# Gathering four blocks at a time instead of three, with two of them by way of DRAM

## The chip, the core and the metric

The kernel runs on one NeuronCore of a Trainium2 chip. The metric is the device time of one launch in microseconds (us). Three runs of the kernel before took 2212.91, 2213.55 and 2214.76 us; the median is 2213.55 us.

## What is computed

The input is x, 4 sequences of 4096 tokens with 192 features, in float32. Three steps follow each other.

```python
# 1. a causal convolution over 7 tokens, weights softmax-normed per head
out[b, s, h, g] = sum_k w[h, k] * x_pad[b, s + k, h, g]
# 2. first network, w_in 192 x 2048 and w_out 2048 x 192
h = x @ w_in;  x = (h - tanh(h)) @ w_out
# 3. second network, other weights of the same sizes
h = maximum(x @ w_in, 0);  out = (h * h) @ w_out
```

All weights and results are wanted to float32 accuracy, so most products are made from parts: a value is split into a rounded high part and the rest, and three matmuls (high x high, low x high, high x low) stand for one product.

## The kernel before

**Blocks and units.** The 16384 tokens are cut into NBLK = 32 blocks of T = 512. The hidden layer of 2048 is cut into 16 tiles of 128 features. A unit (network m, block b, pair p) makes two of the 16 hidden tiles from z, the block's input, and multiplies two hidden tiles of the unit three places earlier (LAG = 3) with the second weights. There are 8 units to a block, and 512 in all. `units` (lines 692 to 698) is their order: blocks 0 and 1 in turn, blocks 2 to 29 one by one, blocks 30 and 31 in turn, then the second network block by block.

**Parts A and B.** The 192 output features are part A (the first 128) and part B (the last DB = 64). Part A goes through the split matmuls inside the units (line 526). Part B is made by plain float32 matmuls (lines 500 and 507) with 64 columns, of which two lie side by side on the engine. They need all 16 hidden tiles of a block in SBUF, so they are gathered: run in one go, after the last unit of a group of blocks.

**Gathering.** The hidden tiles of 128 x 512 float32 (256 KB) lie in a ring of RING = 32 slots, just two blocks' worth. `gather_at` (lines 700 to 705) says after which unit `gathered` (line 1039) comes. Blocks 0 and 1 are gathered in two parts. From then on three blocks make a group, ten groups in each network; blocks 30 and 31 of the second network come at the very end. Of three blocks the first is in `sent_away`: each of its tiles goes to DRAM right after it is made (`send_away`, line 511), and its slot is free again. The other two stay. When the group is complete, `gathered` issues 16 products for the kept pair (`products_b`: one hidden tile of both blocks at a time, line 500). Each frees two slots, into which two tiles of the first block are fetched from DRAM (`fetch`, line 515, DMAs on SP's queue). Eight products follow for the block alone (`products_b_alone`: two hidden tiles of one block at a time, line 507), whose two half sums are then added.

**Finishing.** `finish_b` (line 640) takes a pair's sum out of PSUM into the one ub buffer (by ScalarE in the first network, line 650, by VectorE in the second, line 648) and stores it: one DMA to DRAM as y in the first network (line 654), four DMAs into the output in the second (lines 656 to 659). `finish_b_alone` (line 663) does so for a single block, by a copy, an add and, in the second network, a transposition. The last pair of all is gathered in two pieces of 384 and 128 tokens, and half of its stores go by ScalarE's queue; line 658 picks the pair by its number.

**Order of the work.** The order on each engine is written out ahead by a planner (lines 708 to 1180). Each piece of work is a Job with an engine (PE, DVE, ACT, or SP for DMAs), an assumed time, and the jobs and buffers that it needs. PE's jobs stay in the order in which `build` writes them: each needs the one before it (line 756). `set_late` (line 1112) gives PE's jobs due times from their assumed times and works back from them to the others. `emit_all` (line 1149) then plays the plan through: each engine takes, among what could start soonest, the job with the earliest due time. Each engine, and SP's queue, runs its instructions in that order on the chip.

**Input of a block.** In the first network VectorE convolves block by block (lines 289 to 295), part A for one block and part B for two, and z is split by ScalarE and VectorE (lines 379 to 404); a DMA copies one half of z (line 371). In the second network y is loaded back from DRAM (lines 426 to 432). There are two z buffers.

**Weights.** The weights come as 64-bit floats and are decoded by ScalarE and VectorE (`decode_ops`, line 130). The eight parts of the second network's weights are loaded late (`late_loads`, lines 1093 to 1094): the first after unit 0 of block 28 of the first network, and each further one 3 units later. There are WBUFS = 9 buffers; all but one of the eight wait for one that block 31 of the first network has used for the last time.

Of the kernel before, what the change touches and what calls it, by code (L numbers as in the profile page):

```python
# [34 lines left out]
def conv_mlp_mlp_kernel(ctx: ExitStack, tc: tile.TileContext, x, weight, w_in1, w_out1, w_in2, w_out2, out):  # L35
# [13 lines left out]
    nc = tc.nc  # L49
# [6 lines left out]
    T = 512  # L56
# [583 lines left out]
    def finish_b(m, b, lo=0, hi=T):  # L640
        box = {}

        def take():
            if lo == 0:
                last_ub[:] = [op.tile([P, T], F32, name="ub")]
            ub = box["ub"] = last_ub[0]
            if m:
                nc.vector.transpose(ub[:, lo:hi], acc_b[m, b, lo][:, lo:hi])  # L648
            else:
                nc.scalar.copy(ub, acc_b[m, b, lo])  # L650

        def send():
            if m == 0:
                nc.sync.dma_start(out=far_pair(b), in_=box["ub"])
                return
            for i in range(2):
                for j in range(4, D // 32):
                    q = nc.scalar if b == NBLK - 2 and i else nc.sync
                    store(j, b + i, box["ub"], 32 * (j - 4) + i * DB, q, lo, hi)

        return [take, send]
# [35 lines left out]
    for b in range(NBLK):  # L697
        units += one_block(1, b)
    at = {u: i for i, u in enumerate(units)}
    gather_at = {5: (0, [0, 1], 0, 6), 15: (0, [0, 1], 6, NU)}  # L700
    sent_away = set()
    for m in range(2):
        for b in range(2 - 2 * m, NBLK - 2 * m, 3):
            gather_at[at[m, b + 2, NP - 1]] = m, [b, b + 1, b + 2], 0, NU
            sent_away.add((m, b))
    pairs = [(m, p) for m in range(2) for p in range(NP)]

    class Buffer:
# [163 lines left out]
    def build():  # L872
# [139 lines left out]
                steps_2(k, v, makes, uses, 0)  # L1012
                step.append(pe(lambda k=k, run=run: run(k), 0.2267, wants[k], makes, uses))
        finish(*v[:2], step[5], step[5])
        gathered(1, [NBLK - 2, NBLK - 1], 0, NU)

    def wants_2(wants, v):
        hi, lo_ = ready_w[v[0], v[2]][2:]
# [20 lines left out]
    def gathered(m, blocks, lo, hi):  # L1039
        b = blocks[-2]  # L1040
        ub = Buffer("ub")
        start = len(in_order)
        for piece in [(0, T)] if (m, b) != (1, NBLK - 2) else [(0, LAST), (LAST, T)]:
            share = (piece[1] - piece[0]) / T
            if lo == 0:
                sum_b[m, b] = Buffer("pB")
            q = sum_b[m, b]
            for f in range(lo, hi):
                us = [(m, b + i, f // 2) for i in range(2)]
                needs = [t_done[u, f % 2] for u in us]  # L1050
                if piece[1] == T:
                    free_slots.extend(t_of[u, f % 2].slot for u in us)
                j = pe(lambda f=f, piece=piece: products_b(m, b, f, *piece), 0.8586 * share + 0.19 * (f in (lo, hi - 1)), needs, [] if f else [q], [*(t_of[u, f % 2] for u in us), *([q] if f else [])])
            if hi < NU:
                return
            take, send = finish_b(m, b, *piece)
            j = (dve if m else sca)(take, 0.62 if m else 0.5, [j], [] if piece[0] else [ub], [q, *([ub] if piece[0] else [])])
            y_kept["B", b] = y_kept["B", b + 1] = dma(send, 4 if m else 1, [j], (), [ub])
        if len(blocks) == 2:
            return  # L1060
        a = blocks[0]
        fetched = []
        for f in range(NU):
            t = slot_of_ring()
            fetched.append((dma(lambda f=f, t=t: fetch(m, a, f, t.slot), 1, [away[(m, a, f // 2), f % 2], in_order[start + f // 2]], [t], (), lag=2.5), t))
        q = Buffer("pB")
        for p in range(NP):
            (j0, t0), (j1, t1) = fetched[2 * p : 2 * p + 2]
# [7 lines left out]
            j = dve(turn[0], 0.62, [j], (), [ub])  # L1076
        y_kept["B", a] = dma(send, 2 if m else 1, [j], (), [ub])

    away = {}
    LAST = 384  # L1080
    sum_b = {}
    t_of, t_done, acc_of = {}, {}, {}
# [8 lines left out]
        todo.setdefault(i, []).append(b)  # L1091
    g_bufs = {}
    for n in range(NP, 2 * NP):
        late_loads[at[0, NBLK - 4, 0] + 3 * (n - NP)] = n

    def finish(m, b, done_1, done_0):
        p0, p1 = (acc_of[m, b, i] for i in range(2))
# [113 lines left out]
```

## Time and profile before

| | |
|---|---|
| median of 3 runs | 2213.55 us (2212.91 to 2214.76) |
| profiled execution | 2213.45 us |
| its span, first to last instruction | 2211.7 us |
| PE (TensorE) busy | 2203.8 us |
| DVE (VectorE) busy | 1562.6 us |
| ACT (ScalarE) busy | 1535.0 us |
| moved by DMA | 245.79 MB |

The profile is that of one execution. PE is TensorE's matmuls, PEld its weight loads, SP the engine that issues DMAs; SPq is its queue. A name such as `pB<-ring,wb` says which tile an instruction writes and which it reads; t is a hidden tile in DRAM, ring one in SBUF. L500 is line 500 of the kernel. Each plain float32 matmul stands in the trace as two, so 4 of them make one product of the text.

### The profile page before, as it was taken

To read this page: it belongs to the slowest core of one execution; us is meant where nothing else is said; L and a number is where in the kernel's file an instruction comes from. 1 tells how busy PE (TensorE), PEld (TensorE's weight loads), DVE (VectorE), ACT (ScalarE), POOL (GpSimd) and SP (SyncE) were. 2 spreads that over 40 slices of the span, in tenths; PEclk is the share of its full clock that TensorE was granted. 3 is DMA by queue.
4 is the path that set the end of the run, shared out by engine and by line. 5 is a ranking of instruction groups with operands and counts; after the bars stand their busy time and mean duration, and the time that the engine had idled before them with its cause. 6 is when DMAs were issued, how large, how long until landed. Compare 5 with 4: busy or idle time off the path is not lost.

```text
span 2211.7 us, 45057 instructions
## 1 busy us (share of the span) xinstructions
PE 2203.8 (100%) x17530; PEld 1610.0 (73%) x17530; DVE 1562.6 (71%) x2479; ACT 1535.0 (69%) x2715; POOL 3.3 (0%) x21
## 2 busy tenths in 40 slices
PE   9999999999999999999999999999999999999999
PEld 6786776768686867678786868686867767686867
DVE  9997978879796979698854646464646556464644
ACT  8775766757575757576785858585857668585855
POOL 0000000000000000000000000000000000000000
PEclk9999999999999999999999999999999999999999
DMA  5315243333425241545433332424152433333230
GB/s 145 101 44 186 65 146 110 108 103 106 138 83 158 63 165 46 183 114 180 140 107 108 101 122 87 150 58 165 39 184 69 140 105 99 108 102 125 85 92 16
DMA packets 319549, 245.79 MB, mean 111 GB/s; under 512 B 211853, under 2 KB 219109, under 8 KB 319333
## 3 DMA queue, kind: packets, MB, share of 16 engines
q1 hardware_dynamic: 318245, 242.77, 35.6%
q8 instruction: 137, 2.24, 0.4%
q14 instruction: 79, 0.65, 0.1%
q10 hardware_dynamic: 1088, 0.13, 0.0%
HBM read 125.90 MB, written 109.05 MB: 106 GB/s over the span
## 4 chain that ended last, share of the span: by engine, by line
PE 97%; DVE 1%; DMA 1%; SPq 1%; ACT 0%; issue 0%; DVEq 0%; ACTq 0%
PE ph L526 46%; PE p L526 31%; PE pB L500 13%; PE pB L507 6%; DMA st<-in_moe_w_out 0%; SPq L118 0%; DMA ring<-in_moe_w_in 0%; DVE accA L295 0%; DMA st<-in_moe_w_in 0%; DVE gl L602 0%; DVE ring L585 0%; DVE da L160 0%; DVE accB L295 0%; SPq L285 0%; ACT da L144 0%
## 5 line engine op out<-in xcount | busy, mean ns | idle before, releaser
L526 PE MATMUL ph<-z,w 64*128 64x512 f32 (+1 forms) x9198 | 1747.5, 387 | 1.5 <-DVE z L375 1.0
L526 PEld LDWEIGHTS ph<-z,w 64*128 64x128 f32 (+1 forms) x9198 | 1415.9, 184 | 192.8 <-issue 16.9
L526 PE MATMUL p<-gh,w 64*128 64x512 f32 x4096 | 1255.0, 387 | 0.6 <-DVE w L181 0.6
L602 DVE TENSOR_TENSOR gl<-ring,gh 128x512 fp32r<-128x512 f32 x1024 | 668.9, 687 | 265.8 <-ACT gh L596 247.8
L526 PEld LDWEIGHTS p<-gh,w 64*128 64x128 f32 x4096 | 749.5, 184 | 78.0 <-DVE w L181 1.0
L526 PE MATMUL p<-gl,w 64*128 64x512 f32 x2048 | 788.4, 386 | 0.0
L580 ACT ACTIVATE ring<-ph 128x512 f32<-128x512 f32 x1024 | 607.5, 599 | 218.7 <-PE ph L526 182.8
L596 ACT CAST gh<-ring 128x512 fp32r<-128x512 f32 x1024 | 606.3, 616 | 74.4 <-DVE ring L585 65.1
L526 PEld LDWEIGHTS p<-gl,w 64*128 64x128 f32 x2048 | 375.8, 184 | 38.7 <-DVE gl L602 0.3
L585 DVE TENSOR_TENSOR ring<-ph,ring 128x512 f32<-128x512 f32 x512 | 332.2, 681 | 27.8 <-ACT ring L580 27.2
L500 PE MATMUL pB<-ring,wb 128*64 128x512 f32 (+2 forms) x1472 | 307.8, 575 | 0.0
L500 PEld LDWEIGHTS pB<-ring,wb 128*64 128x64 f32 x1472 | 102.8, 137 | 193.5 <-issue 191.3
L587 DVE TENSOR_TENSOR ring<-ring,ph 128x512 f32<-128x512 f32 x256 | 175.8, 687 | 55.0 <-ACT ring L580 51.5
L668 ACT COPY ub<-pB 64x512 f32<-64x512 f32 x20 | 11.7, 584 | 232.7 <-PE pB L507 231.9
L589 ACT ACTIVATE ring<-ring 128x512 f32<-128x512 f32 x256 | 161.8, 632 | 7.4
L507 PE MATMUL pB<-ring,wb 128*64 128x512 f32 x640 | 140.7, 592 | 0.0
L672 DVE TENSOR_TENSOR ub<-pB,ub 64x512 f32<-64x512 f32 x20 | 13.7, 683 | 171.3 <-ACT ub L668 171.3
L295 DVE SCALAR_TENSOR_TENSOR accA<-xTa,taps,accA 128x512 f32<-128x512 f32 x180 | 133.5, 741 | 0.7
L507 PEld LDWEIGHTS pB<-ring,wb 128*64 128x64 f32 x640 | 46.0, 137 | 91.4 <-issue 83.9
L648 DVE STREAM_TRANSPOSE ub<-pB 128x512 f32<-128x512 f32 (+2 forms) x12 | 8.1, 673 | 108.3 <-PE pB L500 108.3
L295 DVE SCALAR_TENSOR_TENSOR accB<-xTb,taps,accB 128x512 f32<-128x512 f32 x90 | 67.1, 745 | 0.2 <-ACT accB L292 0.2
L388 ACT CAST z<-accA 128x512 fp32r<-128x512 f32 x30 | 18.6, 621 | 54.4 <-DVE accA L295 47.3
(99 smaller groups left out, 474.0 us busy)
## 6 DMA issues: line engine op xcount, KB each, us to landing
t<-ring SPq DMA_DIRECT2D x320, 256.0 KB, 2.1
ring<-t SPq DMA_DIRECT2D x320, 256.0 KB, 5.3
ya<-tu SPq DMA_DIRECT2D x32, 256.0 KB, 2.1
accA<-ya SPq DMA_DIRECT2D x32, 256.0 KB, 2.7
accB<-yb SPq DMA_DIRECT2D x64, 128.0 KB, 2.7
out<-ua SPq DMA_DIRECT2D x128, 64.0 KB, 1.9
xa<-in_x SPq DMA_DIRECT2D x120, 64.0 KB, 2.4
z<-z SPq DMA_DIRECT2D x30, 256.0 KB, 2.9
```

What stands on the lines that cost most here:

```text
L295: nc.vector.scalar_tensor_tensor(a, t[:, k : k + T], w, a, op0=ALU.mult, op1=ALU.add)
L388: nc.scalar.copy(zt[:, 0, 0], acc["A", b])
L500: nc.tensor.matmul(acc_b[m, b, lo][half(i), lo:hi], w, ring_t[m, b + i, f][:, lo:hi], start=f == 0, stop=f == NU - 1)
L507: nc.tensor.matmul(acc_b[m, b, "alone"][half(i)], weights_b(m, p)[:, i], ring_t[m, b, 2 * p + i], start=p == 0, stop=p == NP - 1)
L526: ins = nc.tensor.matmul(o, w, r, start=start, stop=stop).ins
L580: nc.scalar.activation(t, ph, AF.Relu if m else AF.Tanh)
L585: nc.vector.tensor_tensor(t, ph, t, op=ALU.subtract)
L587: nc.vector.tensor_tensor(t, t, ph, op=ALU.mult)
L589: nc.scalar.activation(t, t, AF.Square)
L596: nc.scalar.copy(gh, t_t[m, b, f])
L602: nc.vector.tensor_tensor(gl, t_t.pop((m, b, f)), gh.bitcast(F32), op=ALU.subtract)
L672: nc.vector.tensor_tensor(ub, acc_b[m, b, "alone"][half(0)], ub, op=ALU.add)
```

## The change

Groups have three or four blocks, by the lists N0 and N1. In the first network, from block 2 on, they are 3, then six times 4, then 3; in the second, seven times 4, then 2 and 2. All but the last two blocks of a group are sent away. `gathered` handles the last two as before; one block ahead of them is handled as before; two blocks go to the new `gathered_pair`, which asks for two tiles after each product of the kept pair and then makes 16 products for the fetched pair, in the way of a kept pair, with its own take into ub and its own store. The assumed time of a fetch in the plan rises from 0.55 to 0.66 us. The late loads keep their first place; the second comes after unit 1 of block 29, and each further one 3 units later, which is 6 units later than before for seven of the eight. The constant ENDS replaces NBLK - 2 where the last pair is meant.

```diff
--- before.py
+++ after.py
@@ -655,7 +655,7 @@
                 return
             for i in range(2):
                 for j in range(4, D // 32):
-                    q = nc.scalar if b == NBLK - 2 and i else nc.sync
+                    q = nc.scalar if b == ENDS and i else nc.sync
                     store(j, b + i, box["ub"], 32 * (j - 4) + i * DB, q, lo, hi)
 
         return [take, send]
@@ -697,12 +697,17 @@
     for b in range(NBLK):
         units += one_block(1, b)
     at = {u: i for i, u in enumerate(units)}
+    ENDS = NBLK - 2
+    N0, N1 = [3] + [4] * 6 + [3], [4] * 7 + [2, 2]
     gather_at = {5: (0, [0, 1], 0, 6), 15: (0, [0, 1], 6, NU)}
     sent_away = set()
-    for m in range(2):
-        for b in range(2 - 2 * m, NBLK - 2 * m, 3):
-            gather_at[at[m, b + 2, NP - 1]] = m, [b, b + 1, b + 2], 0, NU
-            sent_away.add((m, b))
+    for m, start, ns in ((0, 2, N0), (1, 0, N1)):
+        for n in ns:
+            blocks = list(range(start, start + n))
+            start += n
+            if m == 0 or start < NBLK:
+                gather_at[at[m, blocks[-1], NP - 1]] = m, blocks, 0, NU
+            sent_away.update((m, b) for b in blocks[:-2])
     pairs = [(m, p) for m in range(2) for p in range(NP)]
 
     class Buffer:
@@ -1012,7 +1017,7 @@
                 steps_2(k, v, makes, uses, 0)
                 step.append(pe(lambda k=k, run=run: run(k), 0.2267, wants[k], makes, uses))
         finish(*v[:2], step[5], step[5])
-        gathered(1, [NBLK - 2, NBLK - 1], 0, NU)
+        gathered(1, list(range(NBLK - N1[-1], NBLK)), 0, NU)
 
     def wants_2(wants, v):
         hi, lo_ = ready_w[v[0], v[2]][2:]
@@ -1040,7 +1045,7 @@
         b = blocks[-2]
         ub = Buffer("ub")
         start = len(in_order)
-        for piece in [(0, T)] if (m, b) != (1, NBLK - 2) else [(0, LAST), (LAST, T)]:
+        for piece in [(0, T)] if (m, b) != (1, ENDS) else [(0, LAST), (LAST, T)]:
             share = (piece[1] - piece[0]) / T
             if lo == 0:
                 sum_b[m, b] = Buffer("pB")
@@ -1056,13 +1061,16 @@
             take, send = finish_b(m, b, *piece)
             j = (dve if m else sca)(take, 0.62 if m else 0.5, [j], [] if piece[0] else [ub], [q, *([ub] if piece[0] else [])])
             y_kept["B", b] = y_kept["B", b + 1] = dma(send, 4 if m else 1, [j], (), [ub])
-        if len(blocks) == 2:
+        alone = blocks[:-2]
+        if len(alone) == 2:
+            gathered_pair(m, alone, start)
+        if len(alone) != 1:
             return
         a = blocks[0]
         fetched = []
         for f in range(NU):
             t = slot_of_ring()
-            fetched.append((dma(lambda f=f, t=t: fetch(m, a, f, t.slot), 1, [away[(m, a, f // 2), f % 2], in_order[start + f // 2]], [t], (), lag=2.5), t))
+            fetched.append((dma(lambda f=f, t=t: fetch(m, a, f, t.slot), FETCH, [away[(m, a, f // 2), f % 2], in_order[start + f // 2]], [t], (), lag=2.5), t))
         q = Buffer("pB")
         for p in range(NP):
             (j0, t0), (j1, t1) = fetched[2 * p : 2 * p + 2]
@@ -1076,7 +1084,29 @@
             j = dve(turn[0], 0.62, [j], (), [ub])
         y_kept["B", a] = dma(send, 2 if m else 1, [j], (), [ub])
 
+    def gathered_pair(m, blocks, start):
+        a = blocks[0]
+        fetched = {}
+        for f in range(NU):
+            for i in range(2):
+                t = slot_of_ring()
+                fetched[f, i] = dma(lambda f=f, b=a + i, t=t: fetch(m, b, f, t.slot), FETCH, [away[(m, a + i, f // 2), f % 2], in_order[start + f]], [t], (), lag=2.2), t
+        q = Buffer("pB")
+        ub = Buffer("ub")
+        for piece in [(0, T)] if (m, a) != (1, ENDS) else [(0, LAST), (LAST, T)]:
+            share = (piece[1] - piece[0]) / T
+            q = Buffer("pB")
+            for f in range(NU):
+                js, ts = zip(*(fetched[f, i] for i in range(2)))
+                if piece[1] == T:
+                    free_slots.extend(t.slot for t in ts)
+                j = pe(lambda f=f, piece=piece: products_b(m, a, f, *piece), 0.8586 * share, js, [] if f else [q], [*ts, *([q] if f else [])])
+            take, send = finish_b(m, a, *piece)
+            j = (dve if m else sca)(take, 0.62 if m else 0.5, [j], [] if piece[0] else [ub], [q, *([ub] if piece[0] else [])])
+            y_kept["B", a] = y_kept["B", a + 1] = dma(send, 4 if m else 1, [j], (), [ub])
+
     away = {}
+    FETCH = 1.2
     LAST = 384
     sum_b = {}
     t_of, t_done, acc_of = {}, {}, {}
@@ -1091,7 +1121,7 @@
         todo.setdefault(i, []).append(b)
     g_bufs = {}
     for n in range(NP, 2 * NP):
-        late_loads[at[0, NBLK - 4, 0] + 3 * (n - NP)] = n
+        late_loads[at[0, NBLK - 4, 0] if n == NP else at[0, NBLK - 3, 0] + 3 * (n - NP) - 2] = n
 
     def finish(m, b, done_1, done_0):
         p0, p1 = (acc_of[m, b, i] for i in range(2))
```

## Rows read from the trace of the kernel before

**Rows 1.** The page: span, busy time by engine, granted clock, chain that ended last.
```profile
span 2211.7 us, 45057 instructions
...
PE 2203.8 (100%) x17530; PEld 1610.0 (73%) x17530; DVE 1562.6 (71%) x2479; ACT 1535.0 (69%) x2715; POOL 3.3 (0%) x21
...
PEclk9999999999999999999999999999999999999999
...
PE 97%; DVE 1%; DMA 1%; SPq 1%; ACT 0%; issue 0%; DVEq 0%; ACTq 0%
...
PE ph L526 46%; PE p L526 31%; PE pB L500 13%; PE pB L507 6%; DMA st<-in_moe_w_out 0%; SPq L118 0%; DMA ring<-in_moe_w_in 0%; DVE accA L295 0%; DMA st<-in_moe_w_in 0%; DVE gl L602 0%; DVE ring L585 0%; DVE da L160 0%; DVE accB L295 0%; SPq L285 0%; ACT da L144 0%
```

**Rows 2.** Chain of waits in order of time: start, length, engine, tile, line, count.
```profile
1293.90 13.88 PE pB L500 x64
...
1307.79 6.87 PE pB L507 x32
...
1396.48 13.88 PE pB L500 x64
...
1410.36 6.87 PE pB L507 x32
...
1704.20 13.88 PE pB L500 x64
```

**Rows 3.** Timeline of PE, 150 to 200 us: the first step of two units.
```profile
152.44 0.39 PE L526 MATMUL p<-gh,w 64*128 64x512 f32 x1
...
162.64 0.39 PE L526 MATMUL p<-gh,w 64*128 64x512 f32 x1
```

**Rows 4.** DMA issues of the page: out<-in, queue, count, KB each, us to landing.
```profile
t<-ring SPq DMA_DIRECT2D x320, 256.0 KB, 2.1
...
ring<-t SPq DMA_DIRECT2D x320, 256.0 KB, 5.3
```

**Rows 5.** Timeline of SP, 164 to 190 us: a gathering's fetches and what follows.
```profile
165.19 8.80 SPq L517 DMA_DIRECT2D ring<-t  x16
...
177.45 0.47 SPq L371 DMA_DIRECT2D z<-z  x1
...
178.73 0.66 SPq L654 DMA_DIRECT2D yb<-ub  x1
```

**Rows 6.** Timeline of SP: an eighth fetch, then sixteenth fetches of four gatherings.
```profile
168.49 0.38 SPq L517 DMA_DIRECT2D ring<-t  x1
...
173.67 0.32 SPq L517 DMA_DIRECT2D ring<-t  x1
...
686.55 0.32 SPq L517 DMA_DIRECT2D ring<-t  x1
...
790.30 0.32 SPq L517 DMA_DIRECT2D ring<-t  x1
...
1713.50 0.32 SPq L517 DMA_DIRECT2D ring<-t  x1
```

**Rows 7.** DMA issues, windows around those five fetches, in that order: us to landing.
```profile
ring<-t SPq DMA_DIRECT2D x1, 256.0 KB, 5.1
...
ring<-t SPq DMA_DIRECT2D x1, 256.0 KB, 5.3
...
ring<-t SPq DMA_DIRECT2D x1, 256.0 KB, 6.5
...
ring<-t SPq DMA_DIRECT2D x1, 256.0 KB, 6.4
...
ring<-t SPq DMA_DIRECT2D x1, 256.0 KB, 5.4
```

**Rows 8.** Stretches: length, busy us (instructions) by engine, PEclk, DMA share, GB/s.
```profile
164.09:184.84 20.75, 20.75 (x98) 6.81 (x97) 13.31 (x21) 5.52 (x11) 0.00 (x0) 1.00 0.69 237
...
184.84:266.66 81.82, 81.82 (x722) 67.36 (x720) 76.50 (x123) 63.01 (x109) 0.11 (x1) 1.00 0.29 83
...
266.66:287.41 20.75, 20.75 (x98) 6.81 (x96) 7.66 (x12) 3.67 (x7) 0.00 (x0) 1.00 0.66 229
...
287.41:369.24 81.83, 81.83 (x723) 67.37 (x721) 77.26 (x125) 63.71 (x113) 0.00 (x0) 1.00 0.31 87
...
676.96:697.71 20.75, 20.75 (x99) 6.80 (x98) 7.65 (x12) 3.67 (x7) 0.00 (x0) 1.00 0.68 228
...
697.71:779.53 81.82, 81.82 (x723) 67.36 (x721) 77.23 (x125) 63.52 (x111) 0.20 (x2) 1.00 0.31 86
...
1005.42:1088.21 82.79, 82.67 (x723) 77.93 (x721) 74.03 (x119) 66.69 (x121) 0.00 (x0) 1.00 0.37 122
```

**Rows 9.** Timeline of all engines, 173 to 202 us: ScalarE's first work after a gathering.
```profile
185.03 0.58 ACT L668 COPY ub<-pB 64x512 f32<-64x512 f32 x1 [6.33 <-PE pB L507]
...
187.92 1.28 ACT L580 ACTIVATE ring<-ph 128x512 f32<-128x512 f32 x2 [2.31 <-PE ph L526]
```

**Rows 10.** Timeline of SP, 950 to 1012 us: loads of the second network's weights.
```profile
974.71 1.65 SPq L118 DMA_DIRECT2D st<-in_moe_w_in  x3
...
985.78 8.96 SPq L517 DMA_DIRECT2D ring<-t  x16
...
1003.81 1.50 SPq L118 DMA_DIRECT2D st<-in_moe_w_in  x3
...
1005.35 0.58 SPq L118 DMA_DIRECT2D st<-in_moe_w_out  x1
```

**Rows 11.** Chain of waits: the weight load that stands on it.
```profile
1005.35 3.29 DMA st<-in_moe_w_out
```

## The prediction

> **What bounds the kernel now.** I read the page first: TensorE (PE) is busy 2203.8 of 2211.7 us at the full granted clock, and the chain that ended last is PE for 97% [rows 1]. So nothing is gained by taking work off VectorE, ScalarE or the DMA engines; the time changes only by what PE issues, or by making PE wait. The chain in order of time shows the rhythm: every three blocks a gathering, 13.88 us of pair products and 6.87 us of products alone, the next one 102.58 us later (1396.48 - 1293.90), with no wait of PE inside or between [rows 2]. The timeline of PE gives one unit as (162.64 - 152.44) / 3 = 3.40 us [rows 3].
>
> **Part 1, fewer gatherings.** One product (two matmuls of the plain kind side by side) costs 6.87 / 8 = 0.859 us [rows 2]. A pair of blocks takes 16 products, a block alone 8, so a block costs 8 however it is gathered and the number of products, 512, stays. What goes is the passage from one kind of matmul to the other and back: 102.58 - 24 units x 3.40 - 24 products x 0.859 = 102.58 - 81.60 - 20.62 = 0.36 us for each gathering. Before there are 2 + 10 + 10 + 1 = 23 gatherings; the new lists give 2 + 8 + 8 + 1 = 19. **Term: 4 x 0.36 = -1.4 us**, on the path itself. The finishing of blocks alone (copy, add, and a transposition in the second network) mostly goes too, on ScalarE and VectorE, beside PE: 0.
>
> **Part 2, twice the fetches in a gathering.** Thirteen gatherings (six in the first network, seven in the second) now fetch 32 tiles of 256 KB instead of 16. Two tiles are asked for after each of the 16 products of the kept pair, into the slots that it frees, and PE needs them two at a time from product 16 on. PE takes its work strictly in the written order, so a tile that is late stops it; nothing stands behind it to fill in. This is the term that decides.
>
> The need: the last product of 32 begins 31 x 0.859 = 26.6 us after the gathering began. The supply: SP sends the 16 fetches within 8.80 us, the first 1.1 us after the start [rows 5, 8]. In the gathering of 164.09 the eighth lands at 168.49 + 5.1 = 173.59 and the sixteenth at 173.67 + 5.3 = 178.97 [rows 6, 7], so one tile every 5.38 / 8 = 0.67 us: the fetches are bound by the DMA engines, not by the issue. The sixteenth lands 14.9 us after the start there, 16.1 us in the gathering of 676.96 (686.55 + 6.5), 17.2 us in that of 779.53 (790.30 + 6.4) and 14.7 us in that of 1704.20 (1713.50 + 5.4) [rows 2, 6 to 8]. Before, this was never a limit, since the last pair of tiles alone is needed only at 23 x 0.859 = 19.8 us, 2.6 us after the latest of these. With 16 more tiles at 0.67 us the thirty-second lands 10.7 us later: at 25.4, 26.8 and 27.9 us for the earliest, a middle and the latest row. Against 26.6 us that is in time, 0.2 us late and 1.3 us late. Less than nothing it can't be, since an early tile does not make PE faster. I take the middle row, the nearest to most gatherings: **term: 13 x 0.2 = +2.6 us**, bounds 0 and 13 x 1.3 = +16.9 us.
>
> Here the Trainium skill speaks against the change: "DMA: Bandwidth & Descriptors", section Bandwidth, says that between HBM and SBUF the HBM side binds at about 358 GB/s. By that a tile would take an estimated 0.73 us and the last would land 1 us later than by the row. The trace does not agree: 256 KB in 0.67 us is 391 GB/s. The same section of the Trainium skill allows a core that streams alone more than that share.
>
> What is queued on SP behind the 32 fetches: the move of z's half and the store of the kept pair's sum, which before left at 177.45 and 178.73 [rows 5], and in the second network the loads of y and four output stores. The planner sorts by due time and the fetches are due first, so all of these leave some 10.7 us later. The moved z belongs to the block after the next, 27 us on: 0. The store must land before the fetched pair's sum can go into the same ub; it is copied by ScalarE or VectorE, which have no other work until about 3 us after PE returns to its units (184.84 to 187.92) [rows 8, 9]: 0, and if that cover is gone, a delay of the first tanh by as much. The 128 more stores to DRAM are sent by SP between other DMAs at a median 2.1 us to landing [rows 4]; the DMA engines are about 30% busy between gatherings [rows 8]: 0.
>
> **Part 3, longer stretches between gatherings.** VectorE is the engine with least room in the first network: 76.50 and 77.26 us of 81.8 between gatherings, 13.31 and 7.66 us of 20.75 inside [rows 8]. Four blocks need 4/6 of the sum of these four, 116.5 us. Of that the gathering takes 13.3 us (as at 164.09, the new gatherings all end on an even block, whose successors share a part-B convolution), which leaves 103.2 of 108.8 us. About 4.6 us of a stretch stay idle now (81.83 - 77.26), so 104.2 are there. It fits with 1.0 us to spare, and the convolution may slip into the longer gathering: 0.
>
> **Part 4, weights of the second network.** Seven of the eight loads move 6 units (20 us) later, past the 32 fetches on SP. Before, loads left at 974.71 and 1003.81, on either side of the fetches at 985.78 [rows 10], and the landing of the last of these stands on the chain for 3.29 us [rows 11]; the stretch after it lasted 82.79 us against 81.82 [rows 8]. The work on each load is the same, and its buffer comes free only when the first network's last block has used it, which stays. **Term: -0.5 us**, bounds -1.0 (the whole excess goes) and +3.3 (a later load is waited for once more, as long as the one on the chain).
>
> **Sum.** -1.4 + 2.6 - 0.5 = +0.7 us. The profiled execution took 2213.45 us (span 2211.7 and 1.75 around it), 0.1 under the median of the runs, 2213.55. I forecast 2214.2 us. A measurement of this kernel tells some 0.2%, 4.4 us, from no change, so this is no change that can be told.
>
> **Rivals.**
> *The stream is late throughout* (slower). The bound of +16.9 is what the latest row gives. For it: the margin is 26.6 against 26.8 us, and a second run of 16 tiles has its own chance of a delay as in the row of 779.53. Against: the row of 1704.20 has 1.2 us to spare. From a mean lateness of (4.4 + 1.9) / 13 = 0.48 us it decides. At 0.9 us the time is 2213.45 - 1.9 + 11.7 = 2223.3 us. Chance 0.27.
> *The DMA engines fall to a lower rate when the stream is twice as long* (slower). The slowest pace in the rows is that of a whole burst with its start, (178.97 - 165.19) / 16 = 0.86 us a tile [rows 5 to 7]. Half-way between it and 0.67, at 0.77 us, the thirty-second lands at 16.1 + 12.3 = 28.4 us, 1.8 late: -1.9 + 23.4, 2235 us. Against it: from the eighth tile to the sixteenth the pace holds. Chance 0.05. The figure of the Trainium skill named above ("DMA: Bandwidth & Descriptors", Bandwidth) is a milder form of this, an estimated 2227 us.
> *VectorE becomes the bound in the first network* (slower). If a gathering takes up only 7.66 us of its work, a stretch needs 108.8 us and has 104.2: 4.6 us in each of six, 2213.45 + 0.7 + 27.6 = 2241.8 us. For it: only 1.0 us is to spare. Against: z of the next block is due only after a gathering that grew by 6.9 us. Chance 0.05.
> *A real gain.* All fetches in time and the whole excess of the weight stretch gone: -1.4 - 1.0 = -2.4 us, 2211.0. That is within 0.2%. To reach -4.4 us something must go that the rows don't show. Chance 0.04.
> That the change does not do what it says could only be through the planner putting other DMAs among the fetches; that is the first rival again.
>
> **How the numbers follow.** The forecast has 0.59, its own range 2211.0 to 2217.9; the three slower cases have 0.37 together. The range reaches down to the best sum, 2211.0, and up over the first rival's 2223.3 to 2224; the two rarer slower cases lie outside. Faster 0.04, same 0.59, slower 0.37.
>
> **What would show it.** In the profile after: 13 gatherings of pair products in two runs, 64 and 64 matmuls, each run about 13.9 us if no tile is late. A longer second run, ended by a fetch, is the first rival, and its excess times 13 is the price. The period of four blocks should be 32 x 3.40 + 32 x 0.859 + 0.36 = 136.6 us. Units longer than 3.40 us late in a stretch, ended by VectorE, are the third. The stretch of blocks 29 to 31 should come nearer to 81.8 us. The prediction is wrong if the gatherings are on time and the sum is still off, or if the sixteenth to thirty-second tiles land at another spacing than 0.67 us.

## The result and the profile after

Six runs of the changed kernel gave 2228.97 us (2225.20 to 2229.93), six of the kernel before beside them 2213.52 us (2212.91 to 2214.81): a ratio of 1.0065 [1.0054, 1.0075], slower by 0.65%. The forecast of 2214.2 us and its range to 2224.0 us were wrong, on the side of the first rival. The profiled execution took 2229.52 us.

From the page of the kernel after: span; busy time; chain by engine; the pair products (busy, mean ns, idle time before them); the fetches.

```profile
span 2227.8 us, 45753 instructions
...
PE 2217.2 (100%) x17530; PEld 1607.8 (72%) x17530; DVE 1544.9 (69%) x2456; ACT 1525.4 (68%) x2701; POOL 3.4 (0%) x21
...
PE 51%; DMA 2%; DVE 0%; issue 0%; ACT 0%; SPq 0%
...
L500 PE MATMUL pB<-ring,wb 128*64 128x512 f32 (+2 forms) x2048 | 444.0, 580 | 1.9 <-DMA ring<-t 1.6
...
ring<-t SPq DMA_DIRECT2D x448, 256.0 KB, 5.4
```

The same 17530 matmuls as before [rows 1], and PE still "busy" for 99.5% of the span; yet PE is busy 13.4 us longer, and DMA has gone from 1% to 2% of the chain, although the chain could be followed back only to 1040 us, over half the span. The group of the pair products shows only 1.6 us of waiting for `ring<-t`. Busy and idle time mislead here: the record of a pair product's matmul is 0.59 us long and the next one starts 0.43 us after it, so that a wait of up to 0.16 us shows as no idle time (the group's 444.0 us are 430.6 where no tile is fetched, in the first experiment below). What tells is the length of a gathering. The thirteen stretches of the kernel after, from the first pair product to the next unit (length, busy time by engine, granted clock, DMA share, GB/s), with their sum:

```profile
294.55:323.18 28.63, 28.32 (x130) 9.20 (x129) 11.21 (x18) 3.69 (x7) 0.00 (x0) 1.00 0.91 312
432.20:461.93 29.73, 29.32 (x130) 9.38 (x128) 11.21 (x18) 3.70 (x7) 0.00 (x0) 1.00 0.87 301
...
984.55:1013.76 29.21, 28.74 (x131) 9.33 (x130) 18.32 (x29) 5.49 (x11) 0.00 (x0) 1.00 0.87 306
...
2055.20:2082.97 27.77, 27.77 (x130) 9.27 (x128) 4.00 (x6) 3.33 (x7) 0.00 (x0) 1.00 0.93 316
sum 374.40, PE 372.51 PEld 121.26 DVE 102.33 ACT 47.22 POOL 0.00; mean PE 28.66 PEld 9.33 DVE 7.87 ACT 3.63 POOL 0.00
```

On time a gathering lasts 27.62 us (shown by the first experiment), so the thirteen are late by 374.40 - 13 x 27.62 = 15.3 us: a mean of 28.80 us, 29.00 in the first network, 28.63 in the second. Where in a gathering the time goes is seen on SP's queue and in the landings. First the timeline of SP in the kernel after at the end of the fetches of 294.55; then DMA issues (count, KB, median us to landing) in windows around four fetches before the tail, the 31st fetch, and the 31st and 32nd fetch and what follows them in the gathering of 1228.38:

```profile
312.31 3.73 SPq L517 DMA_DIRECT2D ring<-t  x6
316.40 0.47 SPq L371 DMA_DIRECT2D z<-z  x1
317.28 7.33 SPq L654 DMA_DIRECT2D yb<-ub  x2
```

```profile
ring<-t SPq DMA_DIRECT2D x4, 256.0 KB, 5.4
...
ring<-t SPq DMA_DIRECT2D x1, 256.0 KB, 6.6
...
ring<-t SPq DMA_DIRECT2D x2, 256.0 KB, 6.9
accA<-ya SPq DMA_DIRECT2D x1, 256.0 KB, 7.2
```

In most gatherings the tiles land 0.67 us apart up to about the 28th, each 5.4 us after its issue, as the prediction had it. The last two to four take 6 to 7.6 us, with gaps of mostly 0.8 to 1.8 us between landings, as soon as the next DMAs are queued: z's move in the first network, the loads of y in the second. The thirty-second tile lands 26.7 to 28.7 us after the start (needed: 26.6). Only in the last of the thirteen do the loads of y leave late, 3.9 us after the last fetch in place of 0.6; it is the shortest, 27.77 us. The sign was there before: z's move leaves 0.7 us after the sixteenth fetches that took 6.5 and 6.4 us to land, but 3.8 us after the one that took 5.3 [rows 5 to 7]. Timeline of SP in the kernel before, behind the first two:

```profile
687.21 0.47 SPq L371 DMA_DIRECT2D z<-z  x1
...
790.99 0.47 SPq L371 DMA_DIRECT2D z<-z  x1
```

The second loss is in the stretch of blocks 29 to 31, 84.37 us against 82.79 [rows 8]. In the kernel after: the stretch, the timeline of ScalarE and VectorE in it, and what PE's weight loads waited for (in all, times, longest).

```profile
1013.76:1098.13 84.37, 82.87 (x722) 69.79 (x721) 73.42 (x119) 67.40 (x123) 0.00 (x0) 1.00 0.41 132
```

```profile
1037.63 0.89 ACT L144 ACTIVATE da<-st 128x768 f32<-128x768 f32 x1 [1.70 <-DMA st<-in_moe_w_out]
...
1038.56 0.63 DVE L152 TENSOR_SCALAR da<-da 128x768 int16<-128x768 int16 x1 [1.90 <-ACT da L144]
```

```profile
PEld ph L526 <- DMA z<-z: 1.3, 1, 1.3
PEld ph L526 <- DVE ring L585: 1.1, 1, 1.1
```

A load of weights lands late, ScalarE waits 1.70 us for it in the middle of its order, VectorE 1.90 us for ScalarE; behind them stand the elementwise work of a unit and the split and move of block 31's z, and PE waits for both. In every profile with the new places this stretch takes 84.1 us or more, in every one with the old places 82.8 or less.

### The profile page after: what moved, and what is told of

The parts are those of the page before. It is cut to its first block, busy times and chain, and to the rows that moved or that the text cites. A ratio compares the mean times of both kernels' runs of the same rounds, so it can differ in the third digit from the quotient of the medians.

```text
span 2227.8 us, 45753 instructions
## 1 busy us (share of the span) xinstructions
PE 2217.2 (100%) x17530; PEld 1607.8 (72%) x17530; DVE 1544.9 (69%) x2456; ACT 1525.4 (68%) x2701; POOL 3.4 (0%) x21
## 4 chain that ended last, share of the span: by engine, by line
PE 51%; DMA 2%; DVE 0%; issue 0%; ACT 0%; SPq 0%
PE ph L526 25%; PE p L526 17%; PE pB L500 10%; DMA ring<-t 1%; PE pB L507 0%; DMA z<-z 0%; DVE ring L585 0%; DVE z L377 0%; DVE gl L602 0%; DVE da L160 0%; ACT gh L596 0%; DVE ub L648 0%; SPq L517 0%; SPq L371 0%
## 5 line engine op out<-in xcount | busy, mean ns | idle before, releaser
L500 PE MATMUL pB<-ring,wb 128*64 128x512 f32 (+2 forms) x2048 | 444.0, 580 | 1.9 <-DMA ring<-t 1.6
L650 ACT COPY ub<-pB 128x512 f32<-128x512 f32 x15 | 8.8, 586 | 111.7 <-DMA yb<-ub 73.3
L623 DVE TENSOR_TENSOR tu<-p,tu 128x512 f32<-128x512 f32 x60 | 41.1, 685 | 4.1 <-PE ph L526 2.5
L616 ACT COPY tu<-p 128x512 f32<-128x512 f32 x60 | 34.9, 582 | 2.7 <-PE p L526 1.8
L627 DVE STREAM_TRANSPOSE ua<-tu 128x512 f32<-128x512 f32 x32 | 22.5, 705 | 0.0
```

What stands on the lines that cost most here:

```text
L500: nc.tensor.matmul(acc_b[m, b, lo][half(i), lo:hi], w, ring_t[m, b + i, f][:, lo:hi], start=f == 0, stop=f == NU - 1)
L616: nc.scalar.copy(tu, acc_t[m, b, 1])
L623: nc.vector.tensor_tensor(box["tu"], acc_t[m, b, 0], box["tu"], op=ALU.add)
L627: nc.vector.transpose(ua, box["tu"])
```

## The experiments

The kernel before took 2214.53 us beside e1 to e4, 2214.35 beside e5 to e8, 2214.22 (one run) beside e9 and e10, and 2214.04 beside e11 to e14. A mean gathering is that of one profiled execution. Where the same DMAs follow in the same way, the mean of a network differs by up to 0.45 us from one profile to the next.

### Is it the fetches at all? (e2_nofetch)

The two blocks' fetches are not sent, and their traffic is gone with them; the products read what lies in the slots.

```diff
-fetched[f, i] = dma(lambda f=f, b=a + i, t=t: fetch(m, b, f, t.slot), FETCH, ...
+fetched[f, i] = dma(lambda f=f, b=a + i, t=t: keep_old(m, b, f, t.slot), FETCH, ...
```

> The changed kernel without the fetches of the pairs: the products of the fetched pair read what the ring slots hold from before, so those outputs are left wrong; PE's work is the same. It leaves the lateness of the fetches out and nothing else. If the fetches are the loss, all gatherings of 32 products take 27.6 us, and the time is that of the kernel before, less 1.4 us for four gatherings, plus 1 to 2 us for the weights: 2213 to 2215 us. If the longer stretches cost anything (VectorE), it stays above 2217 us, with units longer than 3.40 us in the first network.

2214.92 us (2213.81 to 2216.02), ratio 1.0001 [0.9992, 1.0010]. Chain of waits in order of time, two rows (start, length):

```profile
1356.89 27.61 PE pB L500 x128
...
1493.53 27.62 PE pB L500 x128
```

All thirteen gatherings last 27.62 us, and four blocks take 1493.53 - 1356.89 = 136.64 us (forecast: 136.6). The longer stretches and the second pair's handling cost nothing; no unit is late but two in blocks 29 to 31. So the loss comes with the fetches, and besides the weights there is no other.

### Do the DMAs queued behind them slow the last tiles? (e1_hold)

Every other DMA of SP waits, from the first fetch until the 32nd product is done.

```diff
+        for h in holds:
+            if held(j) and j not in h[0] and h[0][0].end is not None:
+                if h[1].end is None:
+                    return None
...
+    gate = nc.sync.nop().ins
+    tc.add_manual_dep(gate, last_b[h[2]], SYNC, reason="after the fetched pair")
```

> The changed kernel, but every other DMA on SP's queue waits from the first fetch of a gathering of two pairs until the matmuls of its thirty-second product are done. Theory 'company': the last two or three tiles of a gathering are slowed by the DMAs that follow them on the queue (they landed 0.8 to 1.8 us apart there, against 0.68 before). Then the last tiles land 0.68 us apart, a gathering takes 27.6 to 28.4 us in place of 27.8 to 29.7, and the time falls by 9 to 13 us, to 2216 to 2220 us. Theory 'pace': 32 tiles at 0.68 us are too many for 26.6 us whatever follows them. Then the gatherings stay at a mean of 28.8 us and the time at 2226 to 2230 us. A third way: the held DMAs are then late themselves, and a gain in the gatherings is lost to waits in the units behind them.

2221.27 us (2220.74 to 2224.60), ratio 1.0031 [1.0019, 1.0043]. Chain of waits:

```profile
1499.48 27.70 PE pB L500 x128
...
1774.57 28.57 PE pB L500 x128
```

The mean of the thirteen is 27.96 us, so 10.9 of the 15.3 us come from what follows the fetches. The rest comes mostly from single gaps: in seven of the thirteen, one tile in the later part of the stream lands 1.3 to 2.2 us after the one before it, the others there 0.6 to 0.7. Holding has a price of its own: the stretches between gatherings are 6.6 us longer in all than on time (1.8 in the kernel after), 4.0 of them in blocks 29 to 31 (86.78 us against 82.79 [rows 8]), where the held DMAs and the weights meet. The profiled execution, 2224.60 us, is the slowest of the six.

### The weights' loads by themselves (e3_wback, e4_wonly, e5_hold_wback)

The kernel after with the loads at their old places; the kernel before with the new places; both mended (e1 with the old places).

```diff
-late_loads[at[0, NBLK - 4, 0] if n == NP else at[0, NBLK - 3, 0] + 3 * (n - NP) - 2] = n
+late_loads[at[0, NBLK - 4, 0] + 3 * (n - NP)] = n
```

> The changed kernel with the loads of the second network's weights at their old places. Theory 'weights': their move puts decoding into the stretch of blocks 29 to 31, where VectorE makes z of block 31 too late; that stretch took 84.4 us against 82.8 before. Then the two waits of 0.8 and 1.0 us there go and the time falls by 1 to 2 us, to about 2227.5 us. Rival: the waits come from the longer group before it (convolutions put off), and the time stays at 2228 to 2230 us. A second rival: loads among the fetches of the gathering after block 28 make its last tiles later still, and the time rises by 1 to 3 us.

> The kernel before with the loads of the second network's weights at their new places, groups of three blocks. Theory 'weights': z of block 31 is late here too, plus 1 to 2 us, 2214.5 to 2215.5 us. Rival (the longer group is needed for it): no change, 2213 to 2214 us, or the 0.5 us less that the prediction expected.

> Held DMAs as in the first experiment, and the weights' loads at their old places: both mended causes together. If the two causes are independent, the gatherings keep a mean of 28.0 us, the stretch of blocks 29 to 31 falls from 86.8 us to 82 to 83 us, and the time falls from 2221.3 to 2216.5 to 2218 us. Compared with the kernel before that is still 2 to 4 us more: 4.5 us of late tiles and two waits of about 1 us in the second network, against 1.4 us saved. If it falls to 2213 us or below, groups of four can be made to pay.

e3: 2227.85 us, 1.0059 [1.0047, 1.0072]. e4: 2216.11 us, 1.0008 [0.9999, 1.0016]. e5: 2217.63 us, 1.0017 [1.0008, 1.0026]. Stretches of e3 (the gathering ahead of blocks 29 to 31, and those blocks), then the same blocks in e4:

```profile
983.79:1013.76 29.97, 29.63 (x132) 9.59 (x130) 22.67 (x35) 7.21 (x13) 0.00 (x0) 1.00 0.94 327
1013.76:1096.02 82.26, 82.26 (x723) 73.15 (x722) 70.88 (x113) 65.86 (x119) 0.00 (x0) 1.00 0.37 116
```

```profile
1007.12:1091.71 84.59, 82.82 (x722) 73.28 (x721) 74.21 (x120) 67.43 (x123) 0.00 (x0) 1.00 0.42 130
```

The later place alone costs 1.8 us of the stretch in the kernel before (84.59 - 82.79 [rows 8]), by the same two waits; the whole time of e4, 1.6 us longer, just fails to show it. The old place in the new kernel has no wait in the stretch, but the gathering ahead of it, where four of the loads now leave just before the fetches, lasts 29.97 instead of 29.21 us. So the new place gains nothing; what it loses net, 1.1 us between the medians of e3 and the kernel after, the intervals do not separate. With the rest held it weighs more: e5 is 3.6 us below e1 in the medians (their intervals just overlap), and blocks 29 to 31 take 82.22 us in it against 86.78. The twelve gatherings of e5 away from the weights have a mean of 27.75 us, 28.77 in the kernel after: what is left when nothing follows is 0.13 us each in this profile, 0.34 in that of e1.

### Which follower? (e6_store_free, e7_store_held)

As e1, but the kept pair's store follows at once; or that store alone is held.

```diff
-        return j.engine == "SP"
+        return j.engine == "SP" and j not in kept_stores   # e6; e7: return j in kept_stores
```

> As the first experiment, but the store of the kept pair's sum is not held: it alone follows the 32 fetches at once. In the first network it is one DMA of 256 KB, in the second four of 64 KB in pieces of 128 bytes. If any follower slows the last tiles, the mean gathering goes from 28.0 back to 28.5 us or more in both networks; if only the move of z and the loads of y do, it stays at 28.0 us. If it is the small pieces, only the second network's gatherings grow.

> The other half: the store alone is held, the move of z (first network) and the loads of y (second) follow the fetches at once. If any follower slows the last tiles: 28.5 us or more in both networks. If the move of z with its rows of 4 KB on half the partitions does, and loads of the fetches' own shape do not: the first network's six gatherings stay near 29.1 us and the second network's seven fall to 28.0 us.

One run each: 2219.35 us and a mean gathering of 27.94 us with the store free; 2228.33 us and 28.59 us with only the store held. The stores, which leave 0.7 us after the last fetch in e6, are harmless; z's move and the loads of y do it. In the second network the store is four DMAs that read 32 partitions each and write to DRAM, so neither the number of followers nor a source of few partitions is enough.

### Would a second queue help? (e8_two_queues)

As e1, with the second block's tiles asked for by ScalarE's queue.

```diff
+fetched[f, i] = Job("ACT" if i else "SP", lambda f=f, b=a + i, t=t, i=i: fetch(m, b, f, t.slot, nc.scalar if i else nc.sync), ...
```

> Held DMAs as in the first experiment, and the fetches of each second block issued by ScalarE's queue, beside SP's. The prediction said that the fetches are bound by the DMA engines and not by the issue. Then the tiles still land 0.68 us apart on the mean and the gatherings stay at 28.0 us, but for what the start gains (tiles 2 and 3 come 1.5 us after the first two). If the issue or a queue's depth is the limit, the spacing falls below 0.6 us, all gatherings take 27.6 us and the time falls by 4 us or more against the first experiment.

2224.04 us, ratio 1.0043 [1.0029, 1.0056]; mean gathering 28.07 us. From the 8th tile to the 28th they land 0.69 us apart in the mean, as in the kernel after. The pace is not set by SP's issue. Once the stream runs, a fetch leaves only when the eighth before it has landed, with one queue or two; more under way was not tried. But the DMA engines have no room in the stream, as a stretch of the kernel after shows (DMA share 1.05, so all 16 are busy, at 387 GB/s):

```profile
302.00:316.00 14.00, 14.00 (x68) 4.64 (x66) 3.76 (x6) 1.82 (x3) 0.00 (x0) 1.00 1.05 387
```

### What in the followers? (e9_accA_only, e10_accB_only)

As e1, but in the second network either the load of y into accA (256 KB, 128 partitions, like a tile) or the two loads into accB (128 KB, 64 partitions each) follow at once.

```diff
+        at_once.add(la)   # e10: lb
...
+        return j.engine == "SP" and j not in at_once
```

> As the held kernel (2221.3 us, mean gathering 27.96 us), but in the second network the load of y into accA, 256 KB on 128 partitions like a fetched tile, follows the fetches at once; the two loads of 64 partitions and the stores stay held. In the first network everything is held. Theory A (any load into SBUF that follows shares the DMA engines with the last fetches): the tail of the second network's gatherings spreads again, the seven gatherings there cost 27.62 + 0.6 to 0.9 us in the mean, those of the first network stay near 27.9 us; about 2223 to 2225 us in all. Theory B (it takes a DMA of 64 partitions, as the move of z and the loads into accB are): the last tiles stay 0.65 us apart, the second network's gatherings stay near 28.0 us; 2220 to 2222 us.

> As the held kernel, but in the second network the two loads of y into accB, 128 KB each on 64 partitions, follow the fetches at once; accA's load and the stores stay held. Theory A (any load into SBUF that follows): the tail spreads as with accA, the seven gatherings of the second network cost 0.6 to 0.9 us over 27.62 in the mean, 2223 to 2225 us. Theory B (it takes 64 partitions): the same here, and not with accA. Theory C (only the number of followers counts, whichever they are): both of these runs show about half the spread.

One run each: 2222.41 and 2221.91 us. DMA issues in a window around the last fetches and the first follower, in the gathering of 1359.63 us of e9, then in that of 1360.32 us of e10:

```profile
ring<-t SPq DMA_DIRECT2D x3, 256.0 KB, 5.3
accA<-ya SPq DMA_DIRECT2D x1, 256.0 KB, 5.2
```

```profile
ring<-t SPq DMA_DIRECT2D x2, 256.0 KB, 6.0
accB<-yb SPq DMA_DIRECT2D x1, 128.0 KB, 5.5
```

Three of the seven gatherings on the chain of waits of e9, then of e10:

```profile
1359.70 28.03 PE pB L500 x128
...
1497.26 27.62 PE pB L500 x128
...
2048.16 27.79 PE pB L500 x128
```

```profile
1360.39 28.19 PE pB L500 x128
...
1497.62 28.00 PE pB L500 x128
...
2047.05 28.44 PE pB L500 x128
```

With accA alone the seven have a mean of 27.86 us; with accB alone, 28.28 us. The time to landing is as clear only in part: three of e9's seven end as shown, with 5.2 to 5.3 us, but in the other four a single gap before the 28th to 30th tile puts off all that follow (6.1 to 6.7 us). From the 28th landing to the 32nd it takes 2.97 us in the mean with accA, 3.53 with accB, 3.04 with both held (e1). The same 256 KB, so it isn't the bytes. By themselves these means differ by no more than those of like profiles can; the next experiments settle it. (The total times are alike only because the waits that holding causes in units differ, 8.1 and 3.2 us.)

### 64 partitions or 128, with nothing held (e11_one_load, e13_pair_load, e14_wide_move)

The kernel after with one edit each: accB filled by one DMA that reads its 64 rows twice (e11); by one DMA of a pair's 128 rows (e13); z moved by a DMA of 128 partitions and twice the bytes (e14), which also has to wait for z's first part. In e13 half of the 128 rows are the other block's; in e14 the move writes the first part over the second.

```diff
-                for i in range(2):
-                    nc.sync.dma_start(out=t[half(i)], in_=far_b(b))
+                nc.sync.dma_start(out=t, in_=bass.AP(y.tensor, y.offset, [[0, 2], *y.ap]))   # e11
+                nc.sync.dma_start(out=t, in_=y_pair[b])                                       # e13
...
-        nc.sync.dma_start(out=zt[half(1 - i), 1].bitcast(F32), in_=zt[half(i), 1].bitcast(F32))
+        nc.sync.dma_start(out=zt[:, 1].bitcast(F32), in_=zt[:, 0].bitcast(F32))               # e14
...
-            cb = lb = dma(move[0], 1, [cb, lb], (), [q], 2.2)
+            cb = lb = dma(move[0], 1, [cb, lb, la], (), [q], 2.2)                             # e14
```

> The kernel after with nothing held; y is loaded into accB by one DMA onto all 128 partitions, which reads the same 128 KB twice, in place of two DMAs of 64 partitions. If it is the 64 partitions of a following load that spread the last fetched tiles: the seven gatherings of the second network fall from a mean of 28.63 us to about 27.9 us, as with accA alone, those of the first network stay at 29.0 us, and the time falls by about 5 us, to 2224 us. If any DMA that follows does it, or the bytes do (they are the same), the second network's gatherings stay near 28.6 us and the time at 2229 us.

> The kernel after with nothing held; for blocks whose part-B sums were stored as a pair, accB is filled by one DMA of 256 KB from the pair's 128 rows, in place of two DMAs of 128 KB onto 64 partitions each: the same bytes, one half of them of the other block, so the values are wrong and the work is the same. If loads onto 64 partitions spread the last tiles: the second network's gatherings fall from a mean of 28.63 us to about 27.9 us, the last tiles' time to landing stays at 5.3 us but for single jumps, the first network stays at 29.0 us, and the time is about 2224 us. If any load that follows does it, the second network stays at 28.6 us and the time at 2229 us.

> The kernel after with nothing held; the move of z in the first network writes all 128 partitions of z's second part from those of the first, 512 KB in place of 256 KB on 64 partitions, so the values are wrong. If 64 partitions spread the last tiles: the first network's gatherings fall from 29.0 us to 27.7 to 28.2 us in spite of twice the bytes, the second network stays at 28.6 us, and the time is 2221 to 2225 us. If bytes that follow do it, or a transfer from SBUF to SBUF as such: the first network's gatherings stay at 29 us or grow, 2229 us or more.

e11: 2225.40 us, ratio 1.0048 [1.0033, 1.0063]. e13: 2225.96 us, 1.0053 [1.0038, 1.0068]. e14: 2232.39 us, 1.0079 [1.0062, 1.0096]. DMA issues at the tail of a second-network gathering in the kernel after (1365.97) and in e13 (1367.34), a window from the last two or four fetches to the first store:

```profile
ring<-t SPq DMA_DIRECT2D x2, 256.0 KB, 6.0
accA<-ya SPq DMA_DIRECT2D x1, 256.0 KB, 6.5
accB<-yb SPq DMA_DIRECT2D x2, 128.0 KB, 5.8
out<-ub SPq DMA_DIRECT2D x2, 64.0 KB, 5.2
```

```profile
ring<-t SPq DMA_DIRECT2D x4, 256.0 KB, 5.3
accA<-ya SPq DMA_DIRECT2D x1, 256.0 KB, 5.3
accB<-yb SPq DMA_DIRECT2D x1, 256.0 KB, 5.3
out<-ub SPq DMA_DIRECT2D x1, 64.0 KB, 4.9
```

Gatherings on e13's chain of waits, second network (plain products are line 505 there), and on e14's, first network:

```profile
1367.41 27.66 PE pB L505 x128
...
1915.06 28.19 PE pB L505 x128
```

```profile
304.52 27.80 PE pB L500 x128
...
989.44 27.77 PE pB L500 x128
```

In e13 the second network's seven fall from a mean of 28.63 to 27.86 us and the first network's stay late (29.27); in e14 the first network's six fall from 29.00 to 27.92 us, though twice the bytes follow, and the second's stay late (28.93). Each edit cures its own network alone, and the followers still leave close behind: z's move 0.7 to 1.0 us after the last fetch in e14, accB's load 1.0 to 1.5 us after it in six of e13's seven. **It is the transfer onto 64 partitions behind the fetches that slows them.** The means of all profiles of fetched gatherings fall apart along this line: 27.7 to 28.2 us for a network where no such transfer follows closely, 28.3 to 29.3 where one does. e14's time went the wrong way for another reason: its first fetched gathering begins at 304.45 instead of 294.55 us. Of those 9.9 us, 5.8 are one wait of PE, and behind it the granted clock is at its lower level (0.50, 1.2 GHz) for 6.8 us, in which matmuls begin 0.43 us apart in place of 0.23: an estimated 3 us more. Why PE waits there was not followed further; it bears on nothing that is compared here. PE's first matmul after the wait in e14, then a stretch behind it (the clock is the third number from the end):

```profile
102.47 0.79 PE L526 MATMUL p<-gh,w 64*128 64x512 f32 x1 [5.79 <-ACT tu L620]
```

```profile
104.00:106.00 2.00, 2.00 (x12) 1.56 (x10) 1.49 (x3) 1.75 (x4) 0.00 (x0) 0.50 0.52 212
```

e11 agrees (a mean of 28.03 us in the second network) but changed two things, as the last section tells.

The Trainium skill has a rule that fits: "SBUF — State Buffer", section "Door 1: The DMA port swizzle", says that 64 partitions of one half reach only 8 of SBUF's 16 DMA ports. The runs agree in direction; how a later transfer on half the ports holds back an earlier one on all of them, none of them shows.

### All mended at once (e12_all_mended)

The single load of accB of e11, the weights' loads at their old places, and only z's move held.

> That single load of accB, the weights' loads back at their old places, and only the move of z held until the fetched pair's products are done; loads of y and stores follow at once. If the 64 partitions are the cause: all thirteen gatherings have a mean of about 27.8 to 27.9 us, no unit waits in the blocks 29 to 31, and the loads of y come without the stalls that holding them caused: 2213.5 - 1.4 + 13 x 0.25 = 2215 us, 2214.5 to 2216.5 us, still not below the kernel before (2214.3 us), since some of the gatherings stay late by single packets of instructions. If bytes or any follower count, the second network stays at 28.6 us: about 2220 us.

2217.83 us (2215.29 to 2218.96), ratio 1.0013 [1.0004, 1.0023]. Twelve gatherings have a mean of 27.88 us; the one before the weights took 30.55 us, where four of their loads leave just ahead of its fetches, the first of which goes 1.8 us after the start in place of 1.1. The time is 2.8 us above the expected 2215. No version tried beats the kernel before; even with every tile on time the gain could only be the 1.4 us of part 1, less than a measurement tells.

## Why the prediction was wrong

**Part 1 was right.** -1.4 us: gatherings on time last 27.62 us and a period of four blocks 136.64 us.

**Part 2 failed, at two steps.** First, "What is queued on SP behind the 32 fetches" was costed at 0 by asking only who waits for those DMAs. It did not ask what they do to the fetches ahead of them on the same queue. So "With 16 more tiles at 0.67 us the thirty-second lands 10.7 us later" took the pace from a gathering whose tail has no close follower: at 164.09 the next DMA, z's move at 177.45 [rows 5], leaves 3.8 us after the last fetch; in the tails of the changed kernel it mostly leaves 0.6 to 0.7 us after it. The pace itself held to about the 28th tile, but the thirty-second lands 27.75 us after the start in the mean; with the followers held (e1), 26.86. That this meets the forecast's 26.8 us is in part luck: the row it starts from, of 676.96, has z's move close behind and so holds some of the delay already (its sixteenth tile lands at 16.1 us, those of e1 at 15.6 in the mean), while the single gaps were not reckoned with. Second, one middle row stood for the mean. Early tiles gain nothing (e1's first gathering has its last tile at 26.0 us and still takes 27.62) and late ones cost, so the spread of the landings around 26.86 us makes 0.34 us a gathering even in e1, not 0.2. What replaced the term of +2.6 us is 15.3 us: a mean of 1.18 us for each gathering, 10.9 us of it by the DMAs behind (e1 against the kernel after; e5 would give them more), the rest mostly by single gaps. The stated bound of +16.9 us covered this; the range stopped at the rival's 0.9 us a gathering.

**Part 3 was right.** VectorE is no bound: in e2 no unit is late outside blocks 29 to 31. The first five gatherings of the first network took up 11.21 us of its work, less than the 13.3 us reckoned, and the stretches between them some 102.7 of 109.0 us, about the 103.2 reckoned.

**Part 4 had the wrong sign.** The term was -0.5 us; the stretch shows +1.6 us, within the bound of +3.3. That "a later load is waited for once more" was the case. What the working lacked is that ScalarE and VectorE run this program in a fixed order, so one late load stops the elementwise work of a unit and the next z behind it, which the chain alone did not show.

**The sum of the spans.** -1.4 + 15.3 + 1.6 = +15.5 us of 2227.8 - 2211.7 = 16.1 us. Another 0.7 us arose ahead of the first pair products (34.11 us from the start, 33.43 before), in a part that the change doesn't touch.

**The rivals.** *The stream is late throughout* is what happened, at 1.18 us and not 0.9, with a cause that was mostly unforeseen: less each burst's own chance of delay than what follows it. *A lower rate in a long stream* is refuted by the 0.67 us that hold to about the 28th tile. *VectorE becomes the bound* is refuted by e2. A *real gain* did not come.

## What to carry to other kernels

When a burst of fetches must land on time, what follows it on its queue counts too: look at the landings of its last tiles in a row that has the same followers, and keep transfers onto 64 partitions from following closely, or make them span all 128. A stalled gathering shows in the length of its stretch, not in the busy or idle time of its group. And with a margin below a microsecond on a strictly ordered engine, thirteen repeats make any small lateness the result, while the gain in sight was 1.4 us.

## What the hardware showed that was not expected

- **A later DMA delays earlier ones.** Fetches take 5.36 us to land in a steady stream at 0.67 us each, so about eight are under way. With transfers onto 64 partitions close behind, the last one took 6.0 to 7.6 us in twelve gatherings of the kernel after; with only 128-partition loads of 256 KB behind (e13, second network), 5.2 to 5.3 where no single gap came just before it and 5.6 to 6.4 where one did.
- **A load that repeats its source is slow.** In e11 accB's 32 loads take 7.4 to 9.7 us to land, between gatherings too; in e13, with the same bytes from 128 rows, they take 2.5 to 2.9 between gatherings. In e11 the store behind accB's load took 8.7 us to land; in e13, 4.9 (shown above). The row of e11:

```profile
out<-ub SPq DMA_DIRECT2D x1, 64.0 KB, 8.7
```

The Trainium skill says why this may be: "DMA: Bandwidth & Descriptors", section "Rules for kernel authors", has it that a leading dimension of c repeated copies confines a DMA to at most c of the 16 engines. The trace agrees: as such a load lands, the semaphore that tells of it is raised twice, and sixteen times for each load of e13. So e11's follower ran on two engines only, as far as this tells, and it is no clean test of the partitions.

- **Single gaps in the stream.** In each gathering of e1 one packet of instructions, 16 KB, passes the DMA engines, and 2 to 3 us later a tile lands 1.1 to 2.2 us after the one before, in all thirteen. Where it comes in the first half, the gathering lasts 27.79 us in the mean (six), in the second half 28.12 us (seven). The row of DMA queues, 1797 to 1801.5 us of e1 (packets, MB, share):

```profile
q8 instruction: 1, 0.02, 1.5%
```

That the packet is the cause was not tried.
